# Decay attention and mixer: 64x64 tiles for the scores of the second blocks, and the form without the upper block from pair 4 on

## The chip, the cores and the metric

The kernel runs on one core of a Trainium2 chip. The metric is the device time of one execution in microseconds. TensorE is called PE here, VectorE DVE, ScalarE ACT, GpSimd POOL; SP is the engine that issues most of the DMAs. PEld is the loading of weights into PE, which overlaps its matmuls.

## The reference, cut to what matters

All is in float32. B = 4, H = 8 heads, S = 768 rows, D = 64.

```python
rel = pos[:, None] - pos[None, :]
Dmask = np.where(rel >= 0, lam ** rel, 0.0)
for b in range(nb):
    intra = einsum('bhic,bhjc->bhij', qb, kb) * Dmask
    intra = einsum('bhij,bhjd->bhid', intra, vb)
    inter = einsum('bhid,bhde->bhie', qb * lam_pow, kv_state)
    out[:, :, sl] = intra + inter
    kv_state = lam_block * kv_state + einsum('bhsd,bhse->bhde', kb_dec, vb)
# x: the heads side by side, (4, 768, 512); then the mixer
h = relu(x.T @ w_tok1) @ w_tok2
u = x + h.T
out = u + relu(u @ w_ch1) @ w_ch2
```

Within a block the scores are causal: what lies above the diagonal is zero. The result does not depend on the length of the block, and the kernel takes 128 where the reference takes 64.

## The kernel before, in words

There are 16 pairs of heads (4 batches, 4 pairs each), and the attention handles one pair after the other, two heads in the two halves of the 128 partitions. A pair has NC = 6 chunks of 128 rows. For a pair the program makes kT and qT (64 dims of each head by 768 rows), the scores of each chunk, their product with the decay mask (mask_scores, on DVE, out of PSUM), the state after each chunk (state: kd times v on PE, a scan on DVE, a placement on POOL), and the outputs (v times masked scores plus state times scaled q), which land transposed in uT.

There are two forms of scores and outputs. In the first, for pairs below NSKIP, the scores of a chunk are one matmul for each head: 64 dims of contraction, 128 keys by 128 queries (L370). All 6 chunks go through two tiles of two PSUM banks, 3 chunks each, and mask_scores multiplies 128x768 elements twice. In the second form (scores_below, outputs_below), for pairs from NSKIP on, the 64x64 block above the diagonal of a chunk is left out. Its group 0 holds the scores of the second 64 queries of each chunk against all 128 keys (128x768 elements through the mask), its group 1 the scores of the first 64 queries against the first 64 keys (128x384 elements; two chunks lie on the two halves of the partitions). The outputs of group 1 need the first 64 rows of v of every odd chunk on the upper half of the partitions; these come by a DMA of their own, vf (load_firsts). The mask for group 1 is put in place by own_blocks, a small POOL copy in each pair of heads. uT is written in even chunks and odd chunks instead of first three and last three.

The order is written out by hand. Iteration i of the loop holds scores(i+1), outputs(i, 0), state(i+1), outputs(i, 1), the making of qT and kT for pair i+2 (turn_q, turn_kr on DVE from pairs 5 and 8 on; turn_k and turn_q_rows on PE before), the transposition of pair i's outputs back for the mixer (turn_back, tiles xp, xhi, xlo), and some groups of token-mixing matmuls (L560 and L597), as many as the table `take` says for that iteration. Then it issues loads on SP, in this order: vf for pair i+2 where that pair has the second form, vn for pair i+3, kn, qn and, from pair 8 on, kr for pair i+4; pieces of the mixer's weights come between. kn, qn, kr and vf have two buffers each, vn has three. kn of pair i is read by turn_k (pairs below 8) and by scale_k (kd: ACT, and POOL for one head below pair 8). qn and kr come in packets of 128 bytes (load_dims), kn, vn and vf in packets of 256 bytes. Each engine works in the order of its program, and so does SP. PSUM gives the loop two two-bank tiles for scores and the like, and four single banks for everything else.

```python
NSKIP = 8
...
rows = slice(0, P) if g == 0 else half_of[n % 2]
js = slice(n * P, (n + 1) * P) if g == 0 else slice(n * P, n * P + C)
qs = slice(n * P + C, (n + 1) * P) if g == 0 else js
```

After the loop come the rest of the token mixing and the channel mixing, which the change does not touch.

Of the kernel before, what the change touches and what calls it, by code (L numbers as in the profile page):

```python
# [22 lines left out]
def kernel(  # L23
# [23 lines left out]
    nc = tc.nc  # L47
    B, H, S, D = q.shape
# [3 lines left out]
    P = 128  # L52
# [29 lines left out]
    def bank(tag, nm, n):  # L82
        if tag == "sh" and spare:
            tag = spare.pop()
        return ps.tile([P, n], F32, tag=tag, bufs={"xT": 1, "sh": 3}[tag], name=nm)

    def two_banks(nm, n):
        t = ps.tile([P, 2, 512], F32, tag="sc", bufs=2, name=nm)
        return t[:, :, 0:n]
# [13 lines left out]

    NQ = 5
    NKD = 8
    NSKIP = 8
    C = P // 2
    half_of = [slice(x * C, (x + 1) * C) for x in range(2)]
    loaded = {}
# [111 lines left out]
    for h in range(2):  # L221
        r = slice(h * D, (h + 1) * D)
        nc.vector.tensor_copy(out=lamp[r, :, 0:1], in_=lamb[r].rearrange("p (a h) -> p a h", h=2)[:, :, h : h + 1])
    n = 1
    while n < P:
        nc.vector.tensor_mul(
            out=lamp[:, :, n : 2 * n], in0=lamp[:, :, 0:n], in1=lamp[:, :, n - 1 : n].broadcast_to([P, NP, n])
        )
        n *= 2
    for p in range(NP):  # L230
        nc.gpsimd.tensor_copy(
            out=keep[:, p, :, 1:], in_=lamp[:, p, P - 1 : P, None].broadcast_to([P, D, NC - 2])
# [4 lines left out]
    kTs, qTs, qss, kds, weights_of = {}, {}, {}, {}, {}  # L237
# [82 lines left out]
    def mask_scores(i, g, pair):  # L320
        p = pairs[i][1]
        if i < NSKIP:
            n, ms = 3, slice(0, P)
        else:
            n, ms = ((NC, slice(C, P)), (NH, slice(0, C)))[g]
        w = ms.stop - ms.start
        if g == 0:
            a = ap.tile([P, 2, n, w], F32, tag="a", bufs=2, name=f"a{i}{g}")
        elif i < NSKIP:
            a = up.tile([P, 2, n, w], F32, tag=("B21h0", "B21l0")[i % 2], name=f"a{i}{g}")  # L330
        else:
            a = ap.tile([P, 2, n, w], F32, tag="a1", bufs=2, name=f"a{i}{g}")
        nc.vector.tensor_mul(  # L333
            out=a,
            in0=pair.rearrange("p h (c i) -> p h c i", i=w),
            in1=mask[:, 2 * p : 2 * p + 2, None, ms].broadcast_to([P, 2, n, w]),
        )
        for h in range(2):
            weights_of[i, g, h] = a[:, h]

    def scores_below(i):


        for g in range(2):
            pair = two_banks(f"sc{i}{g}", (NC, NH)[g] * C)
            for n in range(NC):
                at = n * C if g == 0 else n // 2 * C
                rows = slice(0, P) if g == 0 else half_of[n % 2]
                js = slice(n * P, (n + 1) * P) if g == 0 else slice(n * P, n * P + C)
                qs = slice(n * P + C, (n + 1) * P) if g == 0 else js  # L350
                for h in range(2):
                    r = slice(h * D, (h + 1) * D)
                    nc.tensor.matmul(  # L353
                        out=pair[rows, h, at : at + C], lhsT=kTs[i][r, js], rhs=qTs[i][r, qs], start=True, stop=True
                    )
            if g == 0 or i not in SCAN_FIRST:
                mask_scores(i, g, pair)
        return pair

    def scores(i):  # L360
        if i >= NSKIP:
            return scores_below(i)
        for g in range(2):
            pair = two_banks(f"sc{i}{g}", 3 * P)
            sc = [pair[:, h] for h in range(2)]
            for c in range(3):
                cs = slice((3 * g + c) * P, (3 * g + c + 1) * P)
                for h in range(2):
                    r = slice(h * D, (h + 1) * D)
                    nc.tensor.matmul(  # L370
                        out=sc[h][:, c * P : (c + 1) * P],
                        lhsT=kTs[i][r, cs],
                        rhs=qTs[i][r, cs],
                        start=True,
                        stop=True,
                    )
            if g == 0 or i not in SCAN_FIRST:
                mask_scores(i, g, pair)
        return pair
# [3 lines left out]
    def outputs_below(i, o):  # L383
        b, p = pairs[i]
        st = stb[i % 2]
        if o == 0:
            banks_of[i] = [bank(tag, f"xT{i}{n}", 3 * P) for n, tag in enumerate(("xT", "sh"))]
            for y in range(NH):
                for n in range(2):
                    for h in range(2):  # L390
                        nc.tensor.matmul(
                            out=banks_of[i][n][h * D : (h + 1) * D, y * P : y * P + C],
                            lhsT=firsts[i][half_of[1], h, y, :] if n else vns[i][half_of[0], h, 2 * y, :],
                            rhs=weights_of[i, 1, h][half_of[n], y, :],
                            start=(y == 0),
                            stop=False,
                        )
        xT = banks_of[i][o]
        for y in range(NH):
            c = 2 * y + o  # L400
            for h in range(2):
                nc.tensor.matmul(
                    out=xT[h * D : (h + 1) * D, y * P + C : (y + 1) * P],
                    lhsT=vns[i][:, h, c, :],
                    rhs=weights_of[i, 0, h][:, c, :],
                    start=False,
                    stop=False,
                )
            if c == 0:
                continue  # L410
            for h in range(2):
                nc.tensor.matmul(  # L412
                    out=xT[h * D : (h + 1) * D, y * P : (y + 1) * P],
                    lhsT=st[:, c - 1, h, :],
                    rhs=qss[i][:, c - 1, :],
                    start=False,
                    stop=(y == NH - 1),
                )
        nc.scalar.copy(out=chunks_of(uT[b][:, p], i, o), in_=xT.rearrange("p (y i) -> p y i", i=P))  # L419

    def chunks_of(t, i, g):
        t = t.rearrange("p (c i) -> p c i", i=P)
        return t[:, g::2] if i >= NSKIP else t[:, 3 * g : 3 * g + 3]

    def outputs(i, g):
        if i >= NSKIP:
            return outputs_below(i, g)
        b, p = pairs[i]
        st = stb[i % 2]
        xT = bank("sh" if g else "xT", f"xT{i}{g}", 3 * P)  # L430
        for cg in range(3):
            c = 3 * g + cg
            cs = slice(cg * P, (cg + 1) * P)
            for h in range(2):
                nc.tensor.matmul(  # L435
                    out=xT[h * D : (h + 1) * D, cs],
                    lhsT=vns[i][:, h, c, :],
                    rhs=weights_of[i, g, h][:, cg, :],
                    start=(cg == 0),
                    stop=False,  # L440
                )
            if c == 0:
                continue
            for h in range(2):
                nc.tensor.matmul(
                    out=xT[h * D : (h + 1) * D, cs],
                    lhsT=st[:, c - 1, h, :],
                    rhs=qss[i][:, c - 1, :],
                    start=False,
                    stop=(cg == 2),  # L450
                )
        nc.scalar.copy(out=uT[b][:, p, 3 * g * P : (3 * g + 3) * P], in_=xT)
# [3 lines left out]
    def turn_back(i, g):  # L456
# [9 lines left out]
        for c in range(3):  # L466
            nc.tensor.transpose(  # L467
                out=xp[:, c * P : (c + 1) * P], in_=chunks_of(uT[b][:, p], i, g)[:, c], identity=ident
            )
        cs = slice(g, None, 2) if i >= NSKIP else slice(3 * g, 3 * g + 3)  # L470
        hi = xhi[:, cs, (p % 2) * P : (p % 2 + 1) * P]
# [282 lines left out]
    for i in range(-2, NI):  # L754
        if 0 <= i + 1 < NI:
            pair = scores(i + 1)
# [29 lines left out]
        n = early.get(i, len(work) // 4)  # L786
# [646 lines left out]
    rows = [bank(tag, f"rows{x}", es.stop - es.start) for x, (c, es, tag, _, _) in enumerate(last_pieces)]  # L1433
# [35 lines left out]
```

## Time and profile before

| | us |
|---|---|
| median of 3 runs | 558.64 |
| lowest and highest | 556.69 and 760.41 |
| the profiled execution's own time | 558.01 |
| span of its trace | 556.2 |
| around the span | 1.8 |

The span runs from the first to the last instruction that the trace holds. The attention loop fills its first 160 us or so; the scores of pair i+1 begin iteration i, so that the starts of L370 and L353 cut the trace into iterations. A float32 matmul of the attention stands as two records in the trace; "x24" for 12 matmuls is right.

### The profile page before, as it was taken

What the parts mean: (1) busy time and instruction counts of PE and PEld (TensorE: products, weight loads), DVE (VectorE), ACT (ScalarE), POOL (GpSimd) and SP (SyncE); (2) the same over time, 40 slices, a digit from 0 to 9 for tenths busy, and PEclk for the clock granted to TensorE, in tenths of its full rate; (3) what the DMA queues carried; (4) which work ended last, traced back from release to release, by engine and by line L of the source; (5) the groups of instructions that cost most, each with busy time, mean ns of one, the idle gap of its engine ahead of it and who ended that gap; (6) DMA issues with size and microseconds to landing.
All of it is one profiled execution on the core that took longest, in us unless ns stands there. A gap on an engine that the chain in (4) does not pass through costs nothing.

```text
span 556.2 us, 11599 instructions
## 1 busy us (share of the span) xinstructions
PE 543.7 (98%) x4564; PEld 529.9 (95%) x4564; DVE 434.5 (78%) x657; ACT 247.7 (45%) x499; POOL 283.7 (51%) x260
## 2 busy tenths in 40 slices
PE   5999999999999999999999999999999999999997
PEld 4889998989989999999999999999999999999996
DVE  4787789577686989887888887788687878778894
ACT  3464443336244454444434434444455545445431
POOL 5667553647214374444435354355475656568550
PEclk9999999999999999999999999999999999999999
DMA  9999999998702434271625300014766131230176
GB/s 184 255 202 174 225 184 176 168 179 161 133 2 77 152 132 153 53 266 42 238 85 170 126 27 1 0 22 60 140 151 198 58 113 59 69 121 2 23 153 129
DMA packets 178758, 67.61 MB, mean 122 GB/s; under 512 B 166672, under 2 KB 168976, under 8 KB 178704
## 3 DMA queue, kind: packets, MB, share of 16 engines
q1 hardware_dynamic: 173472, 65.69, 49.6%
q10 hardware_dynamic: 5232, 1.18, 1.0%
q8 instruction: 36, 0.59, 0.5%
q14 instruction: 18, 0.15, 0.1%
HBM read 50.07 MB, written 16.78 MB: 120 GB/s over the span
## 4 chain that ended last, share of the span: by engine, by line
PE 89%; DVE 4%; DMA 3%; SPq 2%; ACT 1%; issue 1%; DVEq 0%
PE po L1148 22%; PE pa L922 12%; PE pc L922 9%; PE pb L922 7%; PE pa L1122 7%; PE pc L1122 5%; PE ph L560 5%; PE pd L922 3%; PE sc L353 3%; PE pu L597 2%; PE sc L370 2%; PE xT L435 2%; PE pu L580 1%; PE xp L467 1%; SPq L118 1%; PE kv L295 1%
## 5 line engine op out<-in xcount | busy, mean ns | idle before, releaser
L1161 DVE TENSOR_TENSOR uT<-po,uT 128x768 f32<-128x768 f32 x57 | 54.2, 952 | 15.6 <-PE po L1148 15.3
L937 ACT ACTIVATE c<-c 128x384 f32<-128x384 f32 x42 | 22.1, 526 | 58.8 <-DVE c L982 33.5
L316 POOL COPY stb<-sv 64x320 f32<-64x320 f32 x32 | 27.2, 848 | 39.9 <-DVE sv L303 38.9
L1128 DVE TENSOR_TENSOR uT<-pa,uT 128x768 f32<-128x768 f32 x36 | 34.3, 954 | 10.5 <-PE pa L1122 9.8
L939 POOL TENSOR_TENSOR h22l<-c,h22h 128x384 fp32r<-128x384 f32 x14 | 14.5, 1032 | 41.5 <-ACT h22h L938 41.5
L1128 DVE TENSOR_TENSOR uT<-pc,uT 128x768 f32<-128x768 f32 x27 | 25.8, 955 | 11.6 <-PE pc L1122 11.6
L333 DVE TENSOR_TENSOR a<-sc,mask 128x768 f32<-128x768 f32 (+1 forms) x32 | 26.0, 850 | 7.5 <-PE sc L370 4.6
L486 POOL TENSOR_TENSOR c1l<-cs,c1h 128x512 fp32r<-128x512 f32 x15 | 19.3, 1298 | 23.1 <-ACT c1h L485 23.1
L1148 PE MATMUL po<-h12h,c 128*128 128x384 f32 x112 | 28.7, 337 | 0.0
L1148 PE MATMUL po<-h11h,c 128*128 128x384 f32 x112 | 28.6, 336 | 0.0
L1148 PE MATMUL po<-h21h,c 128*128 128x384 f32 x112 | 28.6, 336 | 0.0
L1148 PE MATMUL po<-h22h,c 128*128 128x384 f32 x112 | 28.6, 336 | 0.0
L560 PE MATMUL ph<-xhi,w1h 128*128 128x256 f32 x96 | 28.1, 293 | 0.4 <-DVE uT L602 0.4
L560 PE MATMUL ph<-xhi,w1l 128*128 128x256 f32 x96 | 27.1, 282 | 0.0
L560 PE MATMUL ph<-xlo,w1h 128*128 128x256 f32 x96 | 27.1, 282 | 0.0
L282 POOL TENSOR_TENSOR qs<-qT,lamp 128x640 f32<-128x640 f32 x16 | 25.2, 1578 | 0.6
L475 DVE TENSOR_TENSOR xlo<-xp,xhi 128x384 fp32r<-128x384 f32 x32 | 17.6, 551 | 9.5 <-ACT xhi L474 9.5
L486 POOL TENSOR_TENSOR c<-cs,c 128x512 fp32r<-128x512 f32 x10 | 12.9, 1294 | 19.6 <-ACT c L485 19.6
L939 POOL TENSOR_TENSOR h21l<-c,h21h 128x384 fp32r<-128x384 f32 x14 | 17.6, 1257 | 10.1 <-POOL h22l L939 3.9
L939 POOL TENSOR_TENSOR h12l<-c,h12h 128x384 fp32r<-128x384 f32 x14 | 14.5, 1033 | 13.5 <-issue 9.0
L485 ACT CAST c1h<-cs 128x512 fp32r<-128x512 f32 x15 | 9.3, 618 | 26.6 <-DVE cs L659 18.9
L419 ACT COPY uT<-xT 128x384 f32<-128x384 f32 x16 | 7.7, 480 | 28.7 <-PE xT L412 28.7
(409 smaller groups left out, 2031.1 us busy)
## 6 DMA issues: line engine op xcount, KB each, us to landing
raw<-in_moe_w_ch_dram SPq DMA_DIRECT2D x20, 512.0 KB, 3.7
vn<-in_v_dram SPq DMA_DIRECT2D x16, 384.0 KB, 5.7
out_dram<-y SPq DMA_DIRECT2D x104, 48.0 KB, 1.9
qn<-in_q_dram SPq DMA_DIRECT2D x44, 96.0 KB, 3.7
kn<-in_k_dram SPq DMA_DIRECT2D x8, 384.0 KB, 7.2
kr<-in_k_dram SPq DMA_DIRECT2D x32, 96.0 KB, 2.8
dc1h<-c1h SPq DMA_DIRECT2D x4, 768.0 KB, 5.4
dc1l<-c1l SPq DMA_DIRECT2D x4, 768.0 KB, 6.6
```

What stands on the lines that cost most here:

```text
L282: nc.gpsimd.tensor_mul(out=qss[i], in0=qTs[i][:, P:].rearrange("p (c i) -> p c i", i=P), in1=lamp[:, p, None, :].broadcast_to([P, NC - 1, P]),
L316: nc.gpsimd.tensor_copy(out=st[r, :, h, :], in_=sv[r].rearrange("p (e c) -> p c e", c=NC - 1))
L333: nc.vector.tensor_mul(out=a, in0=pair.rearrange("p h (c i) -> p h c i", i=w), in1=mask[:, 2 * p : 2 * p + 2, None, ms].broadcast_to([P, 2 ...
L486: nc.gpsimd.tensor_sub(out=lo, in0=src, in1=hi.bitcast(F32))
L560: nc.tensor.matmul(out=ph, lhsT=w[:, c, fs], rhs=x[:, c], start=(i == 0), stop=(i == 3 * NC - 1))
L922: nc.tensor.matmul(out=to, lhsT=w[:, t], rhs=x[:, t], start=(start and i == 0), stop=(i == 5), skip_group_check=not start,)
L937: nc.scalar.activation(src, src, AF.Relu)
L939: nc.gpsimd.tensor_sub(out=hl, in0=src, in1=hh.bitcast(F32))
L1122: nc.tensor.matmul(out=pair[x][:, t], lhsT=w[:, t], rhs=h, start=(start and i == 0), stop=(i == 2), skip_group_check=not start,)
L1128: nc.vector.tensor_add(out=ub, in0=pair[x], in1=ub)
L1148: nc.tensor.matmul(out=to, lhsT=w[:, jj, t * P : (t + 1) * P], rhs=h, start=(i == 0), stop=(i == 3 * JG - 1))
L1161: nc.vector.tensor_add(out=ub, in0=po, in1=ub)
```

## The change: what it does

Two things. NSKIP goes from 8 to 4: pairs 4 to 7 take the second form too, with vf loads for them, own_blocks four iterations earlier, and the even and odd chunks in uT. And group 0 of scores_below issues two matmuls of 64 keys by 64 queries where it issued one of 128 keys by 64 queries; with 64 dims of contraction each is a 64x64 tile of PE, as group 1's are.

```diff
-    NSKIP = 8
+    NSKIP = 4
...
             for n in range(NC):
                 at = n * C if g == 0 else n // 2 * C
-                rows = slice(0, P) if g == 0 else half_of[n % 2]
-                js = slice(n * P, (n + 1) * P) if g == 0 else slice(n * P, n * P + C)
-                qs = slice(n * P + C, (n + 1) * P) if g == 0 else js
-                for h in range(2):
-                    r = slice(h * D, (h + 1) * D)
-                    nc.tensor.matmul(
-                        out=pair[rows, h, at : at + C], lhsT=kTs[i][r, js], rhs=qTs[i][r, qs], start=True, stop=True
-                    )
+                for j in range(2 - g):
+                    rows = half_of[j if g == 0 else n % 2]
+                    js = slice(n * P + j * C, n * P + (j + 1) * C)
+                    qs = slice(n * P + C, (n + 1) * P) if g == 0 else js
+                    for h in range(2):
+                        r = slice(h * D, (h + 1) * D)
+                        nc.tensor.matmul(
+                            out=pair[rows, h, at : at + C], lhsT=kTs[i][r, js], rhs=qTs[i][r, qs], start=True, stop=True
+                        )
```

## Rows read from the trace of the kernel before

**Rows 1.** The page: busy time by engine, and the DMA slices of 13.9 us each.
```profile
PE 543.7 (98%) x4564; PEld 529.9 (95%) x4564; DVE 434.5 (78%) x657; ACT 247.7 (45%) x499; POOL 283.7 (51%) x260
...
DMA  9999999998702434271625300014766131230176
```

**Rows 2.** Windows by iteration: length, busy PE, PEld, DVE, ACT, POOL, clock, DMA share, GB/s.
```profile
73.61:85.51 11.90, 11.45 (x149) 10.60 (x148) 10.21 (x17) 4.93 (x10) 8.61 (x8) 1.00 1.01 190
85.51:97.20 11.69, 11.27 (x179) 10.52 (x178) 10.42 (x18) 3.51 (x7) 3.54 (x3) 1.00 1.00 179
...
140.48:150.70 10.22, 10.22 (x168) 9.24 (x167) 6.91 (x11) 3.22 (x7) 3.14 (x3) 1.00 0.85 146
```

**Rows 3.** Timeline of PE, pair 4 in the first form: scores, then the outputs' start.
```profile
36.07 1.61 PE L370 MATMUL sc<-qT,kT 64*128 64x128 f32 x24
37.61 0.66 PE L435 MATMUL xT<-a,vn 128*64 128x128 f32 x8
```

**Rows 4.** Timeline of PE, outputs in the first form from their start to what follows.
```profile
75.60 0.66 PE L435 MATMUL xT<-a,vn 128*64 128x128 f32 x8
...
78.74 0.44 PE L597 MATMUL pu<-w2h,hh 128*128 128x384 f32 x1
```

**Rows 5.** Timeline of PE, second form: scores, outputs' start, what follows.
```profile
85.51 2.06 PE L353 MATMUL sc<-qT,kT 64*128 64x64 f32 x48
87.39 0.22 PE L391 MATMUL xT<-a,vn 64*64 64x64 f32 x1
...
90.38 0.45 PE L597 MATMUL pu<-w2h,hh 128*128 128x384 f32 x1
```

**Rows 6.** Chain of waits: start, length, what; 24 records of 64x64 tiles.
```profile
87.58 0.35 PE xT L391 x24
```

**Rows 7.** Groups by shape, up to 230 us: count, busy us, mean ns, the mask's two sizes.
```profile
L333 DVE TENSOR_TENSOR a<-sc,mask 128x768 f32<-128x768 f32 x24 | 22.3, 951 | 7.5 <-PE sc L370 4.6 <-PE sc L353 2.8
...
L333 DVE TENSOR_TENSOR a<-sc,mask 128x384 f32<-128x384 f32 x8 | 4.4, 547 | 0.0
```

**Rows 8.** Timeline of SP: kn of pairs 6 and 7.
```profile
38.52 2.10 SPq L142 DMA_DIRECT2D kn<-in_k_dram  x2
...
45.71 0.74 SPq L142 DMA_DIRECT2D kn<-in_k_dram  x1
```

**Rows 9.** Timeline of SP: vf of pair 10, vn of 11, kn and qn of 12.
```profile
100.39 0.61 SPq L182 DMA_DIRECT2D vf<-in_v_dram  x1
101.09 0.57 SPq L168 DMA_DIRECT2D vn<-in_v_dram  x1
101.75 1.51 SPq L144 DMA_DIRECT2D kn<-in_k_dram  x1
103.31 4.30 SPq L118 DMA_DIRECT2D qn<-in_q_dram  x1
```

**Rows 10.** Timelines of POOL and ACT: the last reads of kn of pairs 5 and 10.
```profile
43.97 1.55 POOL L277 TENSOR_SCALAR kd<-kn,mask 128x320 f32<-128x320 f32 x1
```
```profile
93.24 1.00 ACT L275 ACTIVATE kd<-kn,mask 128x320 f32<-128x320 f32 x2
```

**Rows 11.** Timeline of DVE: kT of pairs 10, 12, 14 and 15.
```profile
91.11 0.94 DVE L259 STREAM_TRANSPOSE kT<-kr 128x768 f32<-128x768 f32 x1
...
115.11 0.98 DVE L259 STREAM_TRANSPOSE kT<-kr 128x768 f32<-128x768 f32 x1 [1.18 <-DMA kr<-in_k_dram]
```
```profile
138.11 0.98 DVE L259 STREAM_TRANSPOSE kT<-kr 128x768 f32<-128x768 f32 x1 [1.83 <-DMA kr<-in_k_dram]
...
147.04 0.98 DVE L259 STREAM_TRANSPOSE kT<-kr 128x768 f32<-128x768 f32 x1 [0.84 <-DMA kr<-in_k_dram]
```

**Rows 12.** Chain of waits after kT of pair 12, up to the scores of pair 12.
```profile
118.73 0.47 DVE uT L602
119.21 0.04 issue
119.25 1.34 PE pu L597 x6
120.59 1.99 PE sc L353 x48
```

**Rows 13.** DMA queues from 54 to 147 us.
```profile
DMA packets 78815, 17.03 MB, mean 183 GB/s; under 512 B 77793, under 2 KB 77793, under 8 KB 78801
```

**Rows 14.** Waits of SP, 120.6 to 147 us: us, times, longest.
```profile
SPq L144 <- ACT B21h L705: 3.6, 1, 3.6
```

## The prediction

> **What bounds the kernel now.** I read the page first, then the windows by iteration, the chain of waits, and the timelines of SP and DVE. On the page PE is busy 98% of the span, and that alone would make every saved PE microsecond a saved microsecond. But the DMA slices stand at 9 through the first nine, some 125 us, which is the attention [rows 1]; after it they are low. So two resources are full at the same time where the change works, and one has to see which ends a wait last. The windows say the same by iteration: PE 11.45 of 11.90 us, DVE 10.21, and the 16 DMA engines at 1.01 of their time; only in the last iterations of the loop the DMA share falls to 0.85 [rows 2]. The clock is 1.00 throughout, so nothing here is a matter of the granted clock.
>
> Three rows of DVE show where the loads end a wait. kT of pairs 12, 14 and 15 began only when kr had landed, after 1.18, 1.83 and 0.84 us of idle DVE [rows 11]. For pair 12 the chain of waits goes from that landing through kT, the evictions behind it on DVE, and the last token-mixing matmuls into the scores of pair 12 at 120.59 [rows 12]. PE hides most of these waits now, since it has filling work; it hides them only as long as it isn't early.
>
> What paces the loads? kn of pair 12 is issued at 101.75 [rows 9] into a tile whose last reader, kd of pair 10, ended at 94.24 [rows 10]; qn and kr of pair 12 go to tiles that were turned by 92.05 [rows 11] and are issued from 103.31 on [rows 9]. The buffers had thus been free for 7 to 11 us. I went through the loads of pairs 8 to 15 in this way: all were free, by 1.9 us for kn of pair 8 and by more than 4 us for the rest. SP issues one DMA behind the other without a pause, and where one takes long (4.30 us for a qn that normally takes 0.5 to 1 [rows 9]) it is behind big transfers. So from about 46 us to 147 us the loads run by themselves, 78815 packets at a mean 183 GB/s from 54 us on [rows 13], and a faster PE doesn't make them come sooner. Only up to kn of pair 7 they are released by the kernel: it is issued at 45.71 [rows 8], 0.19 us after kd of pair 5 ended at 45.52 [rows 10].
>
> **The change part by part: PE.** Scores in the second form take 87.39 - 85.51 = 1.88 us for 24 records of 128 keys and 24 of 64x64 tiles [rows 5]. The same kind of 64x64 tiles, 24 records in L391, take 0.35 us [rows 6]. Group 0 becomes 48 such records, so the scores become 72 records, 3 x 0.35 = 1.05, with a start of 0.05: 1.10 us. That is 0.78 less in each of pairs 8 to 15, 6.2 us in all. In pairs 4 to 7 the scores take 37.61 - 36.07 = 1.54 now [rows 3] and would take the same 1.10: 0.44 less. Their outputs with the state take 78.74 - 75.60 = 3.14 in the first form [rows 4] and 90.38 - 87.39 = 2.99 in the second [rows 5]: 0.15 less. Four pairs give 4 x 0.59 = 2.4 us. PE's sum is 8.6 us less.
>
> A rule speaks against the tiles. In 87.58 to 87.93 the 24 records of L391 follow each other at 0.35/24 = 15 ns [rows 6]. The Trainium skill ("TensorE: Matmul & The Clock Gate", section "Wait — 56ns, not 53.3ns?") says that matmuls start no closer than about 25 ns, however few columns they have. By it 72 records would be 1.8 us, an estimate: next to nothing saved in pairs 8 to 15, and 0.26 lost in each of pairs 4 to 7. The row goes below that floor, so I don't take it.
>
> **DVE.** In pairs 4 to 7 the second mask multiplication has 128x384 elements in place of 128x768, 547 ns in place of 951 [rows 7]: 4 x 0.40 = 1.6 us less. Pairs 8 to 15 keep theirs. **POOL.** own_blocks, 0.3 us a copy, moves from iterations 4 to 7 to iterations 0 to 3; POOL is busy 51% [rows 1], and what hides it there is this idle time; uncovered, it would be 4 x 0.3 = 1.2 us. The ACT copies of the outputs keep their count and size.
>
> **SP and DMA.** Pairs 4 to 7 get a vf load each, issued in iterations 2 to 5 ahead of vn, kn and qn (and kr) of later pairs. On SP one takes 101.09 - 100.39 = 0.70 us [rows 9]; on the DMA engines its 98 KB take 0.54 us at 183 GB/s [rows 13]. Four are 2.1 to 2.8 us. Everything behind them on SP is late by that, less what the waits for kn of pairs 6 and 7 absorb: 0.19 us for pair 7 [rows 8, 10] and, taken as alike, 0.2 for pair 6. That gives 1.7 to 2.4 us; I take 2.0. If the waits absorb the first two loads altogether, and these waits end 0.44 sooner because of pair 4's shorter scores, 2 x 0.54 - 0.44 = 0.6 remain; if nothing is absorbed, 2.8. Nothing before 147 us gives this delay back, since the stream never waits.
>
> **What becomes of the 8.6 us.** The loads of pairs 10 to 15 land at the old times plus 2.0, and PE arrives earlier and earlier. The filling work is dealt out by iteration and the order is fixed on each engine: when DVE waits for kr, the evictions behind it wait too, and PE stands as soon as its four single banks are full. So at pair 12 the whole of the earlier savings is lost: kT ends at 116.09 + 2.0, and the chain behind it [rows 12] follows at the same distance. The same again at pairs 14 and 15. For pair 15 kT ends at 148.02 + 2.0 = 150.0 [rows 11]; behind it come on DVE the evictions of two banks (0.47 each in the chain [rows 12], so about 0.9), and then one group of six matmuls, 1.34 [rows 12]; its scores begin at about 148.02 + 0.9 + 1.34 + 2.0 = 152.3. Before they began at 150.70 [rows 2]. That is 1.6 us late. The scores of pair 15 then take 0.78 less, and after them there is no load that PE waits for: 1.6 - 0.8 = 0.8 us.
>
> The profiled execution is 558.01 us, so my sum is 558.8. The median of the runs shown is 0.6 above it; with such a spread I make no correction.
>
> **The rivals.** (a) PE is the bound after all: then 558.0 - 8.6 = 549.4. For it speaks the 98%; against it the three waits for kr and the buffers that were free for long.
>
> (b) Some of SP's waits are for the kernel. The view of SP's waits names, for instance, 3.6 us in which kn of pair 14 waited for ACT [rows 14]; if such waits are real and not just the last signal before a long issue, the loads move up with PE. If half of the PE saving comes through, 558.0 - 4.3 + 0.8 = 554.5. For it: the wait rows. Against it: that tile's last reader had ended many us before.
>
> (c) Slower: the vf loads cost their full 0.70 on SP, 2.8 us, and the gain in the last scores is lost too, because DVE carries a backlog into the turns of the next stage. Pair 15 then begins 1.6 + 0.8 = 2.4 us late, and the whole is 560.4. It decides where DVE, held by kr of pair 8 at about 69 us, can't catch up in the two iterations behind, which leave it 1.7 and 1.3 us [rows 2]. Against it: DVE does 1.6 us less in pairs 4 to 7.
>
> (d) The tiles don't overlap as in L391, and the scores save nothing; the loads still set the pace: 558.0 + 1.6 = 559.6.
>
> By the Trainium skill's 25 ns, cited above, the scores would be case (d).
>
> **How the numbers follow.** The loads set the pace and are late by 0.6 to 2.8 us: 58%, 558.8, between 557.4 and 559.6. Rival (b) 20%, between 552 and 557; (a) 9%; (c) 9%; (d) 4%. To hold 8 in 10 the range leaves out (a) and the lower end of (b), and ends just above (c): 553.0 to 560.6. A measurement of this kernel tells about 2%, 11 us, from no change; even the whole PE sum is 1.5%. So within 2% has 0.95, and faster and slower by more have 0.03 and 0.02, for something that I haven't seen.
>
> **What would show it.** Scores of the second form as 72 records of 64x64 tiles in about 1.1 us. Idle PE in the attention, where there was next to none, some 8 us in all, most of it ended by DVE evictions or by scores that wait for kT. DVE's waits for kr in pairs 10 to 15 of 1 to 4 us each, in place of 3.8 in all. kr of pair 12 landing at about 117, and the scores of pair 15 beginning at 151 to 152.5. From about 160 us on the same lengths as before. The prediction is wrong if the kr loads land earlier than before in the second half of the attention, or if PE stays without idle time there.

## The result and the profile after

The changed kernel takes 563.13 us (median of 6 runs, 560.22 to 590.95) beside 557.09 (6 runs, 556.03 to 760.41) of the kernel before: a ratio of 1.0108, 95% interval 1.0089 to 1.0128, or 6.0 us. The executions of 590.95 and 760.41 us belong to a second, slower state and are not in the ratio. The forecast was 558.8 us, with a range of 553.0 to 560.6. The profiled execution took 562.43 us, 4.4 more than the one of before.

The page of the changed kernel, as [rows 1]; after busy time by engine come the slices of PE, of its clock and of the DMA engines.
```profile
PE 538.0 (96%) x5044; PEld 523.2 (93%) x5044; DVE 433.1 (77%) x657; ACT 247.5 (44%) x499; POOL 283.1 (50%) x260
...
PE   5999977999899999999999999999999999999996
...
PEclk9999999899999999999999999999999999999999
DMA  9998989988802254172634310004766121230275
```
PE is busy 5.7 us less in a span that is 4.4 us longer. Where the DMA slices stand at 8 and 9, the sixth and seventh slices of PE fall to 7, and the eighth slice of the clock is 8.

Windows of the changed kernel: the iterations of [rows 2], then a stretch of 3.4 us within the second of them.
```profile
72.87:88.06 15.19, 11.33 (x196) 9.73 (x196) 14.59 (x25) 4.89 (x10) 8.05 (x6) 1.00 1.08 193
88.06:102.50 14.44, 12.11 (x204) 11.14 (x203) 10.18 (x19) 3.39 (x7) 3.15 (x3) 0.88 1.00 174
143.16:155.41 12.25, 9.82 (x192) 8.62 (x191) 7.02 (x11) 3.22 (x7) 3.20 (x4) 1.00 0.72 125
...
98.50:101.90 3.40, 3.15 (x15) 3.11 (x15) 2.70 (x6) 1.07 (x3) 0.00 (x0) 0.50 0.89 146
```
The first iteration took 11.90 us before and takes 15.19, with PE's busy time nearly as it was (11.33 beside 11.45) and 3.9 us of idle PE; here DVE is busy 14.59 of the 15.19 us. The last took 10.22 with PE busy throughout and takes 12.25, with 2.4 us of idle PE.

PE's timeline of the changed kernel, second form, as [rows 5]: the scores and what follows them.
```profile
53.14 1.28 PE L354 MATMUL sc<-qT,kT 64*64 64x64 f32 x72
54.24 0.22 PE L392 MATMUL xT<-a,vn 64*64 64x64 f32 x1
```
The 72 records take 1.10 us from start to start, as forecast.

DVE's timeline of the changed kernel, kT of pairs 8, 10, 12, 14 and 15, as [rows 11].
```profile
71.84 0.98 DVE L259 STREAM_TRANSPOSE kT<-kr 128x768 f32<-128x768 f32 x1 [2.74 <-DMA kr<-in_k_dram]
95.45 0.98 DVE L259 STREAM_TRANSPOSE kT<-kr 128x768 f32<-128x768 f32 x1 [2.51 <-DMA kr<-in_k_dram]
119.37 0.98 DVE L259 STREAM_TRANSPOSE kT<-kr 128x768 f32<-128x768 f32 x1 [1.54 <-issue]
140.08 0.98 DVE L259 STREAM_TRANSPOSE kT<-kr 128x768 f32<-128x768 f32 x1 [0.36 <-DMA kr<-in_k_dram]
151.73 0.98 DVE L259 STREAM_TRANSPOSE kT<-kr 128x768 f32<-128x768 f32 x1 [3.10 <-DMA kr<-in_k_dram]
```
SP's timelines: the four issues of kr of pair 8 and of pair 15, in the changed kernel, then before.
```profile
66.01 2.23 SPq L118 DMA_DIRECT2D kr<-in_k_dram  x4
...
144.71 3.42 SPq L118 DMA_DIRECT2D kr<-in_k_dram  x4
```
```profile
63.38 2.23 SPq L118 DMA_DIRECT2D kr<-in_k_dram  x4
...
141.89 2.18 SPq L118 DMA_DIRECT2D kr<-in_k_dram  x4
```
The chain of waits of the changed kernel around the same loads.
```profile
91.02 4.35 DMA kr<-in_k_dram
95.45 0.98 DVE kT L259
...
98.79 3.77 PE ph L561 x18
...
138.60 2.16 PE ph L561 x18
...
147.61 4.00 DMA kr<-in_k_dram
151.73 0.98 DVE kT L259
152.71 0.44 DVE uT L603
153.15 0.48 DVE xlo L476
153.67 0.55 PE xp L468 x3
154.22 1.26 PE pu L598 x6
155.48 1.21 PE sc L354 x72
```
Three things are to be seen. First, the kernel's end hangs on kT of pair 15. It began at 147.04 before [rows 11] and begins at 151.73, 4.69 us later, after DVE stood 3.10 us for its load. Its scores follow 3.68 us behind it, before 3.66; and from their start to the end of the span it is 405.2 us, before 405.5. So the loss of this execution lies ahead of kT of pair 15, and the wait that ends last there is the one for the load. (Without this wait kT could have begun at 148.63, still 1.59 us later than before.)

Second, the lateness of the load has two parts. kr of pair 8 was issued 2.63 us later than before and kr of pair 15 2.82 us later, so that between the two the stream of loads took 78.7 us, before 78.5. But from the first issue of kr of pair 15 to its kT it was 7.02 us, before 5.15: another 1.87.

Third, the 18 matmuls at 98.79 took 3.77 us where the same 18 take 2.16 at 138.60: the granted clock of [98.5, 101.9] is 0.50, the lower of the two levels (1.2 GHz of 2.4). Ahead of it PE had stood still for 2.07 us, waiting for DVE behind kr of pair 10. Idle times of 2.32 us ahead of 81.90 and of 2.23 ahead of 153.67 in the same trace were followed by no such stretch.

### The profile page after: what moved, and what is told of

It reads as the page before. It is cut to its first block, busy times and chain, and to the rows that moved or that the text cites. A ratio compares the mean times of both kernels' runs of the same rounds, so it can differ in the third digit from the quotient of the medians.

```text
span 560.6 us, 12572 instructions
## 1 busy us (share of the span) xinstructions
PE 538.0 (96%) x5044; PEld 523.2 (93%) x5044; DVE 433.1 (77%) x657; ACT 247.5 (44%) x499; POOL 283.1 (50%) x260
## 4 chain that ended last, share of the span: by engine, by line
PE 78%; DMA 8%; DVE 5%; SPq 5%; issue 1%; ACT 1%; POOL 0%; ACTq 0%; DVEq 0%
PE po L1149 21%; PE pa L923 12%; PE pc L923 9%; PE pb L923 7%; PE pa L1123 7%; PE pc L1123 5%; SPq L118 5%; DMA qn<-in_q_dram 3%; PE ph L561 3%; PE pd L923 3%; DMA kr<-in_k_dram 3%; PE pu L581 1%; DMA uT<-in_moe_w_tok_dram 1%; PE sc L354 1%; PE pu L598 1%; PE xT L413 1%
## 5 line engine op out<-in xcount | busy, mean ns | idle before, releaser
L333 DVE TENSOR_TENSOR a<-sc,mask 128x768 f32<-128x768 f32 (+1 forms) x32 | 24.3, 798 | 4.6 <-PE sc L371 4.2
L420 ACT COPY uT<-xT 128x384 f32<-128x384 f32 x24 | 11.5, 478 | 28.7 <-PE xT L413 28.7
L413 PE MATMUL xT<-qs,stb 128*64 128x128 f32 x240 | 21.7, 274 | 0.0
```

The lines of the kernel that those rows point to most:

```text
L413: nc.tensor.matmul(out=xT[h * D : (h + 1) * D, y * P : (y + 1) * P], lhsT=st[:, c - 1, h, :], rhs=qss[i][:, c - 1, :], start=False, stop=( ...
```

## The experiments

My theory after this: the load stream sets the pace, and the four vf loads and something else make it late. Rivals: the saved PE time itself does harm (idle spells, then the low clock), or the tiles do by their shape. All runs are beside runs of the kernel before on the same chip, whose medians were 557.7 to 558.0 us. A difference in us below is the ratio less 1, times that median. None of them reaches 2%; what is called slower or faster has an interval that leaves out 1.

| kernel | us, median (runs) | ratio to before, 95% | PE records |
|---|---|---|---|
| e1 tiles alone | 561.79 (10) | 1.0057 [1.0027, 1.0087] | 4756 |
| e2 border alone | 563.72 (6) | 1.0103 [1.0062, 1.0144] | 4756 |
| e3 four unread loads | 560.10 (10) | 1.0039 [1.0009, 1.0069] | 4564 |
| e4 change without its loads | 562.18 (10) | 1.0063 [1.0038, 1.0088] | 5044 |
| e5 tiles, issued twice | 563.89 (4) | 1.0106 [1.0074, 1.0139] | 5140 |
| e6 tiles, long padding | 561.02 (6) | 1.0062 [1.0039, 1.0085] | 4820 |
| e9 tiles, fitting padding | 560.85 (12) | 1.0040 [1.0006, 1.0073] | 4788 |
| e8 16 KB more per pair | 561.23 (10) | 1.0055 [1.0016, 1.0094] | 4564 |
| v1 tiles, no vf loads | 560.77 (10) | 1.0051 [1.0030, 1.0072] | 4772 |
| v2 change, no vf loads | 565.49 (4) | 1.0144 [1.0102, 1.0187] | 5068 |
| v3 first form in all pairs | 553.35 (4) | 0.9921 [0.9901, 0.9942] | 4180 |
| v4 border at 12, tiles | 555.32 (7) | 0.9945 [0.9920, 0.9971] | 4468 |
| v5 border at 12, no tiles | 555.07 (6) | 0.9949 [0.9932, 0.9967] | 4372 |

**The change in parts.** e1 is the diff without its first hunk, e2 that hunk alone.
```diff
-    NSKIP = 4
+    NSKIP = 8
```


> Only the 64x64 tiles; pairs 4 to 7 stay in the first form, no added loads. If the loads set the pace: PE's 6 us in pairs 8 to 15 are waited away, kr lands as in the kernel before, and only the last scores show: 0 to 1.5 us faster than before. If PE set the pace: 6 us faster. If the tiles themselves cost something: slower.

> Only the second form from pair 4 on, with the old 64x128 matmuls. If the loads set the pace: the four added loads make all later ones late as in the changed kernel, 4 to 6 us slower than before. If the tiles were the cause: as before, within 1 us.

Each part alone is slower, by 3.2 us and 5.8 us (e2 has the four loads and as many more records as e1). The two don't add up: their sum is 9.0 us, the whole change 6.0. For e1 nothing of the loss was in my sum: it has not one load more, and PE's scores in pairs 8 to 14 fell from 14.8 to 9.3 us of busy time. Its trace has kT of pair 15 at 150.69, 3.65 us later than before, and two stretches at the low clock. The second comes after the last wait for a load. Windows of e1:
```profile
119.50:122.90 3.40, 3.40 (x14) 3.31 (x13) 2.81 (x7) 1.00 (x2) 0.60 (x1) 0.50 1.05 147
153.60:157.00 3.40, 3.40 (x85) 2.96 (x87) 1.60 (x3) 0.10 (x1) 0.00 (x0) 0.50 0.00 1
```
A busy stretch of 3.4 us at half clock does the work of 1.7 us at full clock. Less than that shows in the time: from kT of pair 15 to the end of the span it is 409.6 us in e1, 408.9 in the changed kernel, whose clock is 1.00 there, and 409.2 before. So the second stretch accounts for some 0.7 us of the 4.1 by which e1's profiled execution was longer than that of before, and the later kT for the rest (3.65, of which the shorter scores give 0.3 back).

**The loads alone.** e3 adds four vf loads that nobody reads to the kernel before; e4 takes those of pairs 4 to 7 out of the changed kernel (these pairs read a constant tile in place of their vf, so that part of their output is left out).
```diff
+        elif 4 <= i + 2 < NSKIP:
+            load_extra(i + 2)
```
```diff
-        if NSKIP <= i + 2 < NI:
+        if i + 2 == NSKIP:
+            firsts[4] = ap.tile([P, 2, NH, D], F32, tag="vf", bufs=2, name="vf4")
+            nc.gpsimd.memset(firsts[4], 0.1)
+        elif NSKIP < i + 2 < 8:
+            firsts[i + 2] = firsts[4]
+        elif 8 <= i + 2 < NI:
             load_firsts(i + 2)
```


> The kernel before with four vf loads more, of pairs 4 to 7, at the places on SP where the change puts them; nobody reads what they bring. If the loads' price alone is the cause: 3 to 5 us slower than before, kr of pair 15 issued about 4 us later. If the second form's computation in pairs 4 to 7 is the cause: within 1 us of before.

> The changed kernel without the four added loads: pairs 4 to 7 read one constant tile in place of their rows of v, so that the outputs of the odd chunks' first halves are others. If the loads are the cause: at the time before or up to 2 us faster. If the second form's computation is: 4 to 6 us slower than before, as the changed kernel.

Four loads cost 2.2 us (0.5 to 3.8), 0.55 each, less than the 3 to 5 that were expected. Without them the change is still 3.5 us slower (2.1 to 4.9), between the two answers expected. 2.2 and 3.5 make 5.7, close to the 6.0 of the whole: the loads are a good third of the loss, and the rest came with what e4 keeps, the tiles and the second form in pairs 4 to 7. Of e2's 5.8 us the loads likewise leave 3.6 that nothing here takes apart. One of its six executions had a clock of 1.000, and it took 560.87 us, the least of the six; e3's median is 560.10.

**Giving PE its time back.** e5 issues each matmul of the second blocks in group 0 twice over the same result. e6 and e9 put long matmuls ahead of them, whose results are overwritten.
```diff
 # e5
+                        for _ in range(2 - g):
 # e9 (e6: both groups, w = 384 and 96)
+            for h in range(2 - 2 * g):
+                r = slice(h * D, (h + 1) * D)
+                w = 280
+                nc.tensor.matmul(
+                    out=pair[:, h, :w], lhsT=kTs[i][r, :P], rhs=qTs[i][r, :w], start=True, stop=True
+                )
```


> The 64x64 tiles in pairs 8 to 15 (the border left at 8), with every matmul of the second blocks issued twice, the second time over the same result: TensorE gets back the 0.7 us per pair that the tiles saved. Theory A (the saved time turns into idle spells, after which the granted clock falls to half for 3.4 us): no idle spell of 2 us or more is left before 150 us, the clock stays at 1.00, and the time is that of the kernel before, 557 to 559.5 us (ratio 0.998 to 1.003). Theory B (the 64x64 tiles themselves delay the loads or the other engines, idle or not): the time stays at that of the tiles alone, 561 to 563 us, and the scores of pair 15 start at 154 us or later.

> The 64x64 tiles in pairs 8 to 15 as in the tiles alone, with TensorE's saved time given back by four long matmuls per pair ahead of the second blocks (their results are overwritten), where the doubled kernel gave it back by 24 short ones: TensorE's time as before, 256 records more than before in place of 576. Theory C (TensorE's instructions are loaded over the same DMA engines as q, k and v, 16 KB and about 0.9 us of the load stream for each 128 records or so): two instruction loads more than before, 559 to 560.5 us, 3 us or more under the doubled kernel's 563.89. Theory B (the tiles delay something by their shape): 562.5 to 565 us, as the doubled kernel. If only the clock's fall counted in the tiles alone: 557.5 to 558.5 us.

> The 64x64 tiles in pairs 8 to 15 with two long matmuls per pair (overwritten) that give TensorE back the 0.8 us per pair that the tiles saved: 224 records more than before, a little under two instruction loads. If only idle spells and the clock's fall made the tiles slower: 557 to 558.5 us. Theory C (each instruction load of 16 KB costs the load stream 0.7 to 0.9 us, and TensorE may wait for it): 559 to 560.5 us. If the tiles' shape delays something: 561.5 us or more.

In e5 the scores of seven pairs take 14.8 us of busy PE again, as before, and the clock is 0.998 or more in all four executions; yet it is the slowest of the three, 5.9 us behind before and above both times that were expected. So something other than the clock slows e5. In its trace kT of pair 15 begins at 151.32 without waiting for its load: here PE was late. Its waits of PE, 50 to 170 us, name what is new:
```profile
PE xT L414 <- issue: 1.3, 1, 1.3
PE xT L404 <- issue: 1.1, 1, 1.1
PE xT L393 <- issue: 0.7, 2, 0.5
...
PE kv L295 <- issue: 0.6, 1, 0.6
```
3.7 us in which PE stood in the middle of a run of matmuls, and no signal that the profile shows ended the wait. Its timeline at the second of them, and the DMA queues shortly before:
```profile
135.03 0.45 PE L404 MATMUL xT<-a,vn 128*64 128x64 f32 x6
136.62 0.22 PE L404 MATMUL xT<-a,vn 128*64 128x64 f32 x1 [1.14 <-issue]
```
```profile
q1 hardware_dynamic: 1421, 0.18, 92.8%
q8 instruction: 1, 0.02, 6.1%
```
The packets of the queue "instruction" (q8) go with the number of PE's instructions: 33 of them for 4180 matmul records (v3), 36 for 4564 (before), 39 for 5044 (the changed kernel), 40 for 5140 (e5). The page of the kernel before gives them 0.59 MB, 16 KB each; the one here, in a window of 1.2 us, took 6.1% of 16 engines, 1.17 us on one engine. Taken packet by packet, every such stop of PE between 54 and 160 us, of any kernel here, ends 1.2 to 1.6 us after an instruction load ended:
```
kernel  load ended   PE goes on   (us)
e5       87.60        89.11
e5      111.10       112.65
e5      135.28       136.62
e5      147.08       148.38
e5      158.23       159.79
e4       66.72        68.18
e4      144.55       145.89
e1      110.53       111.97
r1      112.47       113.89
e9      145.04       146.37
after   146.00       147.22
v2       68.65        70.02
v2      129.57       130.95
```
They occur only in kernels with the tiles: none in before and its repeat, e2, e3, e8, v3 and v5; and not in all of those, for e6, v1 and v4 have none. The reading that fits all 13 is that PE had run out of instructions: it had gone through 16 KB of short matmuls before the next 16 KB had come over the full DMA engines. e9 differs from e5 in how the time is given back (0.67 us a pair, by long matmuls), with 352 records less. It is 3.7 us faster and has one of those stops, of 0.3 us. So the tiles' shape isn't what makes e5 slow. e9 is still 2.2 us (0.3 to 4.1) behind before: its trace has kT of pair 15 at 150.86, after DVE waited 2.36 us for the load. Its clock was 0.998 or more in 7 of 12 executions, and these took a median 559.3 us, the other five 561.1. e6 was a miss as a test: its padding took 9.7 us of busy PE in seven pairs, nearly twice what the tiles had saved, and its trace has no wait for kr, so PE's own work can explain its 3.5 us.

**Where the loads are late.** e8 puts a row of 16 KB into the stream for each of pairs 4 to 15 (12 of them, into a part of the output that is written again later). Two repeated traces say how far a load's time varies.
```diff
+        if 4 <= i + 2 < NI:
+            load_row(i + 2)
```


> The kernel before with one more transfer per pair in SyncE's stream for pairs 4 to 15, a single row of 16 KB that nobody reads (into a part of the output that is written again at the end): twelve packets of the size of an instruction load. If such a packet holds one DMA engine for over a microsecond and the stream waits for the slowest engine (theory C), each costs 0.6 to 1.2 us: 565 to 572 us, less if the transfers are split into small packets. If one engine's delay is made up by the others: 557.5 to 560 us.

> The tiles alone again, for its trace: if the lateness of the loads is a matter of the instruction count, the last issue of kr falls 1 to 4 us after that of the kernel before again (144.5 to 147.5 us); if it was that execution's, it may fall anywhere from 142.5 us.

> The kernel before again, for its trace: the last issue of kr at 143 to 144.5 us if the stream repeats within a microsecond, up to 146 us if it varies by as much as the tiles' lateness.

The row was carried as 16 packets of 1 KB, so it is not an instruction load's double. It shows what a mere 16 KB cost in this stream: 3.1 us for 12 (0.9 to 5.2), 0.26 each, where 98 KB cost 0.55; the time lies between the two that were expected. The repeated executions took 560.58 us (tiles) and 563.38 (before). kT of pair 15, first in e1, then its repeat, then the repeat of before:
```profile
150.69 0.98 DVE L259 STREAM_TRANSPOSE kT<-kr 128x768 f32<-128x768 f32 x1 [2.21 <-DMA kr<-in_k_dram]
```
```profile
149.19 0.98 DVE L259 STREAM_TRANSPOSE kT<-kr 128x768 f32<-128x768 f32 x1 [2.38 <-DMA kr<-in_k_dram]
```
```profile
149.33 0.98 DVE L259 STREAM_TRANSPOSE kT<-kr 128x768 f32<-128x768 f32 x1 [1.72 <-DMA kr<-in_k_dram]
```
Before had it at 147.04 in one execution and at 149.33 in the other. The last issue of kr, which the expectations name, fell at 143.55 before and at 146.36 in its repeat; at 147.35 with the tiles and at 145.66 in their repeat; at 147.61 in the changed kernel. A lateness of 2 to 3 us in a single trace thus proves nothing, and whether the tiles delay the loads can't be told from these. e6, with the tiles and 38 instruction loads, issued it at 144.89. The repeat of before also has the low clock, behind 1.9 us of idle PE:
```profile
152.50:159.30 6.80, 6.80 (x100) 6.13 (x100) 2.41 (x4) 0.00 (x0) 0.00 (x0) 0.50 0.01 2
```
What is different is how often. The mean clock of an execution was 0.998 or more in 68 of 75 executions of before; in none of 11 of the tiles alone (0.992 to 0.996); and in 17 of 22 with the time given back (e5, e6, e9). Of before the four lowest, all 0.994, took 563.0 to 565.4 us, where the median of their session was 557.7. But the low clock isn't needed for the loss: the one execution of the changed kernel at 0.998 took 562.58 us and the one of e4 at 0.999 562.55, as much as the others.

**Without vf loads.** v1 and v2 make vf on the chip: a matmul with the identity moves the first 64 rows to the upper half of the partitions, and ACT copies them. v3 sets the border at 16, so that no pair needs vf (its second masked scores go to another buffer); v4 and v5 set it at 12.
```diff
+        nc.tensor.matmul(
+            out=at[high].rearrange("p (h y d) -> p h y d", h=2, d=D), lhsT=ident[low, low],
+            rhs=vns[i][low, :, 1::2, :], start=True, stop=True,
+        )
+        nc.scalar.copy(out=vf[high].rearrange("p h y d -> p (h y d)"), in_=at[high])
```


> The 64x64 tiles in pairs 8 to 15, and the eight small loads of second halves of v replaced by one matmul with the identity and one ScalarE copy each. If the loads alone set the pace: eight loads at the 0.55 us that the four unread ones cost are 4.4 us, so 553 to 555 us. If the clock's fall counts too (theory A): the loads run ahead, TensorE idles less, and the time is 554 to 557 us. If neither the loads nor the clock matter: 561 us as with the tiles alone.

> The whole change (tiles, border at pair 4), with the twelve small loads of v replaced by one matmul with the identity and one ScalarE copy each. If the loads alone set the pace: as the kernel with the border at 8 and no such loads, 553 to 555 us, since the saved 1.6 us of VectorE count only where it is late. Theory A: 553 to 558 us, by whether idle spells remain. If the added loads had no part in it: 562 to 563 us.

> The first form of the scores in all sixteen pairs, so that none of the small loads of v is issued, and no 64x64 tile. If the loads alone set the pace: 4.4 us less than before, 553 to 555 us. If VectorE's masks (about 0.4 us more for each of eight pairs, 3.2 us) count in full: 556 to 559 us. Theory A: the clock stays at 1.00, since TensorE saves only some 1.5 us.

> The change with its border at pair 12: first form in pairs 0 to 11, 64x64 tiles in pairs 12 to 15, so that four small loads of v are left and TensorE has 3620 matmuls in place of 3668 before and 3476 with the first form everywhere. Theory C: the loads end some 3 to 4 us later than with the first form everywhere, which had about 4 us to spare at pair 15, and the last four pairs save 0.6 us of TensorE's time each, 2.4 us: 551 to 554 us. If TensorE's saving never counts: 553.5 to 556 us.

> The border at pair 12 with the 64x128 second blocks of before. TensorE's time in the last four pairs is then within 0.4 us per pair of the first form's. Theory C: 552.5 to 555.5 us, level with the first form everywhere or up to 2 us later; 1 to 3 us slower than the same border with tiles if TensorE sets the pace there, level or faster if the loads do.

v1 missed by 3 us and more: the matmuls with the identity took 6.0 us of busy PE in seven pairs, all that the tiles had saved; its loads were early, but PE no longer had time for that. v2 missed as well; its trace has stops for instructions of 2.3 and 1.3 us, and from 130.5 on 6.8 us at a clock of 0.50. v3 is the best of all, 4.4 us faster than before. Its timeline and windows (last line: the iteration that ends with the scores of pair 15, as in [rows 2]) show why:
```profile
141.80 0.94 DVE L259 STREAM_TRANSPOSE kT<-kr 128x768 f32<-128x768 f32 x1
```
```profile
72.69:84.33 11.64, 10.98 (x125) 10.16 (x124) 10.60 (x17) 4.82 (x10) 8.02 (x6) 1.00 0.94 183
...
136.66:146.37 9.71, 9.71 (x120) 9.10 (x119) 7.37 (x11) 3.22 (x7) 3.38 (x4) 1.00 0.46 85
```
kT of pair 15 begins 5.2 us earlier than before [rows 11] and waits for no load; PE is busy all of the last iteration, and the DMA engines are half idle. Eight loads are gone, and 384 PE records with them (33 instruction loads in place of 36). A third thing goes with them: by [rows 3 to 5] the first form takes 1.54 + 3.14 us of PE for a pair's scores and outputs, the second of before 1.88 + 2.99, so that PE saves some 0.2 us in each of eight pairs, 1.5 us in all, and PE is what bounds v3's last iteration. Which of the three gives how much isn't separated. v5 lies between, with half of the loads. v4 adds the tiles to v5 and gains nothing by them (555.32 and 555.07), though 2 us had been hoped for.

## Why the prediction was wrong

Right: that the loads set the pace, and what the parts take by themselves. The scores became 72 records in 1.10 us. PE's busy time fell by 5.7 us, and would have by some 7.3 without the slow stretch (3.77 - 2.16); 8.6 were forecast. PE's saving became waits: DVE stood 8.7 us for kr in pairs 8 to 15, in place of 3.85. The price of the vf loads was right too: 2.0 us forecast, 2.2 measured (e3). And at pair 14 the sum still holds: kT began 1.97 us later than before (140.08 beside 138.11).

Rival (a) is out, since the kernel became slower with less PE work. Rival (b) is out: in the changed kernel no issue of kr from pair 8 on came earlier than before. Rival (d) is out: 72 records in 1.10 us are 15 ns each. The Trainium skill ("TensorE: Matmul & The Clock Gate", section "Wait — 56ns, not 53.3ns?") has matmuls start no closer than about 25 ns; this trace goes below that. Rival (c) came nearest, and its condition was met: DVE waited 2.74 us for kr of pair 8 and was busy 14.59 of the next 15.19 us. But that backlog was gone by pair 14, and e1, with none of its loads, is slower too.

Wrong: the step "The same again at pairs 14 and 15. For pair 15 kT ends at 148.02 + 2.0 = 150.0". In the profiled execution kT of pair 15 was not 2.0 but 4.69 us late. The first issue of kr makes 2.82 of this, at the upper end of what was reckoned (2.8). The other 1.87 lie between that issue and kT, 7.02 us in place of 5.15, and the sum has no term for them. This stretch took 6.06 us in the repeat of before, 5.00 and 5.20 with the tiles alone and 6.84 in e4, so that it may be this execution's and not the change's. Three smaller points: from the end of kT to the scores 2.24 us were reckoned, and it took 2.70, before 2.68. Of the 0.78 that the last scores saved, only 0.3 reached the end. And "Nothing before 147 us gives this delay back" doesn't hold: kr of pair 9 was issued 5.39 us later than before (77.59 beside 72.20), kr of pair 14 only 2.15 (134.72 beside 132.57).

The medians, which no single execution decides, put the error in one term: PE's part. The sum takes PE's saving ahead of pair 15 as lost without harm and gives 0.8 us for the last scores; lateness comes from the four vf loads alone. Measured, e1, which has PE's saving from the tiles and none of the loads, is 3.2 us slower, and e4, the change without its loads, 3.5.

How PE's part costs this is not shown. Two things that I had excluded were seen. First, I wrote "nothing here is a matter of the granted clock". Behind some of PE's waits of about 2 us and more the clock was at 0.50 for a stretch, in every execution of the tiles alone by their mean clock. But in the changed kernel's trace the one such stretch, at 98.5, was made up by pair 14, and in e1's the last one shows as some 0.7 us. Second, I priced matmuls by their time in the array. Their instructions have to be loaded, 16 KB for some 128 records, over the engines that I had called full, and the stops of PE that end behind such a load come to 3.7 us in e5, but to only 0.2 in the changed kernel's trace.

Open: what makes up the 3.2 and 3.5 us. e9 against e1 gives the idle spells and the clock 1.0 us, with intervals that overlap widely. That the further instruction loads make the stream late is a guess: e8's 0.26 us for 16 KB would make it under 1 us for the changed kernel's three, its stream took 78.7 us from pair 8 to pair 15 beside 78.5 before, and the repeated traces vary by more.

## What to carry to other kernels

Where a stream of loads sets the pace, don't take time saved on the engine that looks full as neutral at worst: here it turned into idle spells, at times followed by the low clock, and the kernel became slower. Look for what takes work off the stream instead: the form with more DVE work but without the small loads was 0.8% faster. And count the instructions that a finer tiling adds as transfers. Repeat the trace of the kernel before, too: a wait that moves by 2 us in one pair of traces may have moved by itself.

## What the runs showed of the hardware

- PE's instructions came as packets of 16 KB, one for 127 matmul records or so (36 packets for 4564 records), 1.17 us of one DMA engine; all 13 stops of PE without a signal ended 1.2 to 1.6 us after such a packet.
- After 2.07 us of idle PE the clock stood at 0.50 in [98.5, 101.9] of the changed kernel; it stayed at 1.00 behind 2.32 us ahead of 81.90 in the same trace and behind 2.08 us ahead of 118.14 in e9. Idle time of this size alone doesn't decide it.
- 72 records of 64x64 tiles in float32 took 1.10 us from start to start, 15 ns each.
- In a full stream a load of 98 KB cost 0.55 us of the kernel's time (e3), one of 16 KB still 0.26 us (e8).
